# Raw weight loads on ScalarE's DMA queue, truer prices in the planner, and the last output tile in halves

## The chip, the cores and the metric

The kernel runs on one core of one Trainium2 chip. The metric is the device time of one execution in microseconds; three runs of the kernel before took 892.23, 892.72 and 895.94 us, so its median is 892.72. A core has TensorE (PE in the profile: matmuls from SBUF into PSUM; PEld is its weight load), VectorE (DVE), ScalarE (ACT), GpSimd (POOL) and SyncE (SP, which here only issues DMAs). All work in parallel, each through its own instructions in order; semaphores tie them together.

## The reference

Three blocks in a row, all in fp32. The attention output of 4 x 576 = 2304 tokens and 512 channels is the input of a gated feed-forward, and that one's output is the input of a second feed-forward.

```python
scores = (q @ k.T) / 8                   # 4 batches, 8 heads, 576 x 576, head width 64
# heads 0-3: a key counts if 0 <= i - j < 32; heads 4-7: if j <= i and j % 32 == i % 32
attn = softmax(where(mask, scores, -1e9)); x = attn @ v          # x: 2304 x 512
xn = x / sqrt(mean(x * x) + 1e-6) * rms_g
g = xn @ w_gate                          # 512 x 1536
x = (g * sigmoid(g) * (xn @ w_val)) @ w_out                      # 1536 x 512
h = x @ w_in                             # 512 x 2048
return (max(h, 0) + log1p(exp(-abs(h)))) @ w_out2                # 2048 x 512
```

The weights arrive as 64-bit floats, which the kernel reads as raw 64-bit words.

## The kernel before

**Attention.** Heads are taken in pairs, and a pair's queries in two units. For each pair one DMA loads queries and keys (`qk`, line 550) and one the values (`vb`, line 564). A unit's scores are matmuls on 64 rows of the array (lines 590 and 603), then come the maximum on VectorE (618), the exponentials on ScalarE (646, 650, 654), sums and reciprocals on VectorE (664 to 666), a transpose on TensorE (692), its eviction (292 on ScalarE or 289 on VectorE) and the product with the values (746). Only two `vb` and three `qk` buffers exist, so a load waits until TensorE has read the old content.

**Weights.** Every 128 x 512 block of raw 64-bit words is loaded into one of two `raw` buffers (`decode`, line 389) and made into fp32: ScalarE converts the high words (390), ScalarE or VectorE the low ones (391 or 393), VectorE joins them in two steps (395, 398). There are 74 such blocks, 512 KB each. Most results are stored to DRAM (`w_kept`, 402) and fetched again later (405). Each fp32 block is split into a rounded part (428, 448 on ScalarE) and a rest (374 on VectorE, 375 on GpSimd); a product of two split operands takes three matmuls (`mm3`, line 457).

**Feed-forwards.** Token columns are cut into chunks of 512 (the last of 256). The products of the first feed-forward run between the attention matmuls; later parts use a scheme of seven products for a 2 x 2 block. `out1` (994) and `out2` (1012) add products into the token store `xs`; the last round of `out2` stores each 128 x 512 output tile (1014).

**Order.** Nothing here is executed in the order of the program text. Each operation is added to a list with an engine, a price in ns and what it reads and writes; an alternative engine has its own price. `Trial.run` plays the list through with these prices, `emit` takes the best of 8 such trials by its own count, and the instructions of all engines are issued in the order of the begin times found there. A different price thus changes the order of everything behind it. A raw load counts as work of the engine SP in this plan (`dma`, line 298: 650 ns), and `AHEAD` and `FAR` hold back loads. TensorE's work has kinds (`mode`: 0 full matmuls, 1 and 3 on a part of the rows, 2 transposes); `LEAVE` is the number of ns by which other work must be more urgent before TensorE leaves the kind it is in for another, except between 0 and 2, where `LEFT` counts.

Of the kernel before, what the change touches and what calls it, by code (L numbers as in the profile page):

```python
# [16 lines left out]
AF = mybir.ActivationFunctionType  # L17
ALU = mybir.AluOpType
# [38 lines left out]
FAR, AHEAD = 12000, 1000  # L57
TURNS, KEEP, SWITCH, LEAVE = 8, 0.5, 125, 4000

# [199 lines left out]
def attn_glu_softplus(  # L259
# [113 lines left out]
    def two(eng, n, name, o, x, y, r, w):  # L373
        pr.add("DVE", 68 + n / 0.96, lambda: getattr(nc.vector, name)(o, x, y), r, w,  # L374
               alt=(110 + n * 2.3, lambda: getattr(nc.gpsimd, name)(o, x, y)))

# [5 lines left out]
    def decode(src, t, kt, keep):  # L382

        raw, kraw = raws.next()
        u, ku = cvu.next()
        words = raw.bitcast(U32).rearrange("p (n two) -> p n two", two=2)
        wlo, whi = words[:, :, 0], words[:, :, 1]
        quarters = raw.bitcast(U16).rearrange("p (n four) -> p n four", four=4)
        dma(340, lambda: nc.sync.dma_start(out=raw, in_=src), hold, [kraw])
        act(512, lambda: nc.scalar.activation(t, whi.bitcast(F32), AF.Copy, scale=2.0 ** -112), [kraw], [kt])  # L390
        pr.add("ACT", 15 + 512 / 0.98, lambda: nc.scalar.activation(  # L391
            u, quarters[:, :, 1], AF.Identity, bias=low, scale=2.0 ** -13), [kraw, all_of("eps")], [ku], alt=(68 + 512 / 1.5,
            lambda: nc.vector.tensor_scalar(out=u, in0=wlo, scalar1=29, scalar2=None,
                                            op0=ALU.logical_shift_right)))
        dve(512, lambda: nc.vector.scalar_tensor_tensor(
            out=u, in0=t.bitcast(U32), scalar=0x80000000, in1=u, op0=ALU.bitwise_and, op1=ALU.bitwise_or),
            [kt, ku], [ku])
        dve(512, lambda: nc.vector.scalar_tensor_tensor(  # L398
            out=t.bitcast(U32), in0=t.bitcast(U32), scalar=3, in1=u,
            op0=ALU.logical_shift_left, op1=ALU.bitwise_or), [kt, ku], [kt])  # L400
        if keep >= 3 * AGAIN:
            dma(170, lambda: nc.sync.dma_start(out=wk[keep], in_=t), [kt], [("wk", keep, keep + 1)])
# [4 lines left out]
    def prep_in(i, rows, sums, all4, eng):  # L407
# [25 lines left out]
        if sums:  # L433
            q = [(w32[:, k * 256:(k + 1) * 256], ("w32", k * 256, k * 256 + 256)) for k in range(4)]
            for o, name, a, b in ((3, "tensor_add", 2, 3), (2, "tensor_sub", 0, 2), (0, "tensor_sub", 3, 0),
                                  (1, "tensor_sub", 1, 0)):
                two("DVE", 256, name, q[o][0], q[a][0], q[b][0], [q[a][1], q[b][1]], [q[o][1]])
            part(1024, 512, 1024, eng)
            part(1024, 0, 512, eng)
# [67 lines left out]
    def attention(at, use):  # L507
# [62 lines left out]
        def stage_s(u):  # L570
# [51 lines left out]
            elif not late(u):  # L622
                dve(6, lambda: nc.vector.tensor_scalar(out=m, in0=m, scalar1=-SCALE, scalar2=None, op0=ALU.mult),
                    [km], [km])
# [13 lines left out]
        def stage_e(u):  # L638
# [8 lines left out]
            else:  # L647
                for a in range(n):
                    if mid(u):
                        pr.add("ACT", 60 + nk / 0.98, lambda a=a: nc.scalar.activation(  # L650
                            ev[:, a, :], sv[:, a, :], AF.Exp, bias=m[:, a:a + 1], scale=SCALE),
                            [kb_, km, all_of("table")], [(ke[0], a * nk, a * nk + nk)])
                        continue
# [8 lines left out]
        def stage_p(u, n, nk, loc, t0, e, ke, ev, z, kz):  # L662
            if whole(u) or mid(u):
                dve(n * nk, lambda: nc.vector.reduce_sum(out=z, in_=ev, axis=AX.X), [ke], [kz], lock=False)
            dve(6, lambda: nc.vector.tensor_scalar_add(out=z, in0=z, scalar1=1e-9), [kz], [kz])
            dve(30, lambda: nc.vector.reciprocal(out=z, in_=z), [kz], [kz], lock=False)
# [40 lines left out]
        def turned(xb, kx, n, nq):  # L707
            xv = xb[:, :n * 65].rearrange("p (a c) -> p a c", c=65)
            z, (kz, _, _) = mz.next()
            z, kz = z[:, 1, :n], (kz, 0, 10)  # L710
            dve(6, lambda: nc.vector.tensor_scalar_add(out=z, in0=xv[:, :, 64], scalar1=1e-9), [kx], [kz])
            dve(30, lambda: nc.vector.reciprocal(out=z, in_=z), [kz], [kz], lock=False)
# [283 lines left out]
    def out2(fs, g, first, c, j, last):  # L996
        ti = CUTS[c] // 128 + j
        ts = slice(j * 128, (j + 1) * 128)
        pb, kp = o_banks.next()
        pairs = []  # L1000
        for f in fs:
            i = f % 4
            st, km = g[f, c]
            pairs.append(([x[:, ts] for x in st], [wout[i][:, x, :] for x in (0, 1)],
                          lambda a, b, i=i, km=km: [(f"wout{i}", b * 512, b * 512 + 512), km[a]]))
        mm3(pb, kp, pairs, DM)
        o = ti * DM
        x, kx = xs[:, o:o + DM], ("xs", o, o + DM)
        if first:
            act(DM, lambda: nc.scalar.activation(x, pb, AF.Copy), [kp], [kx])  # L1010
        else:
            dve(DM, lambda: nc.vector.tensor_add(x, pb, x), [kp, kx], [kx])  # L1012
        if last:
            dma(256, lambda: nc.sync.dma_start(out=out[ti * 128:(ti + 1) * 128, :], in_=x),
                [kx], [("out", ti, ti + 1)])

# [320 lines left out]
```

## Time and profile before

| | |
|---|---|
| median of three runs | 892.72 us (892.23 to 895.94) |
| the profiled execution | 897.35 us, its span 895.6 us |
| TensorE matmuls | busy 880.6 us (98%) |
| VectorE | busy 717.6 us (80%) |
| ScalarE | busy 509.8 us (57%) |
| GpSimd | busy 62.9 us (7%) |
| DMA | 102.31 MB, mean 114 GB/s, all on one queue but 0.9 MB |

The span is from the first to the last instruction of the program; the execution's time has a little around it. Busy time of TensorE is modelled from pipelined matmuls, so a busy TensorE can still be slowed down, by a low granted clock for one. Register, branch, semaphore and DMA-issuing instructions do not count as busy: SyncE has no busy time at all, and its waits are seen in its issues. A wait in a row stands in square brackets: how long the engine was idle and what ended it.

### The profile page before, as it was taken

What the parts mean: (1) busy time and instruction counts of PE and PEld (TensorE: products, weight loads), DVE (VectorE), ACT (ScalarE), POOL (GpSimd) and SP (SyncE); (2) the same over time, 40 slices, a digit from 0 to 9 for tenths busy, and PEclk for the clock granted to TensorE, in tenths of its full rate; (3) what the DMA queues carried; (4) which work ended last, traced back from release to release, by engine and by line L of the source; (5) the groups of instructions that cost most, each with busy time, mean ns of one, the idle gap of its engine ahead of it and who ended that gap; (6) DMA issues with size and microseconds to landing.
All of it is one profiled execution on the core that took longest, in us unless ns stands there. A gap on an engine that the chain in (4) does not pass through costs nothing.

```text
span 895.6 us, 14064 instructions
## 1 busy us (share of the span) xinstructions
PE 880.6 (98%) x5350; PEld 729.5 (81%) x5350; DVE 717.6 (80%) x1326; ACT 509.8 (57%) x967; POOL 62.9 (7%) x59
## 2 busy tenths in 40 slices
PE   8889999999999999999999999999999999999998
PEld 7667778787878888888888888887888888888886
DVE  5988999897699997888899798977799457676644
ACT  3977766664364677565665478544473655434331
POOL 1210212310012000000000010000000000000000
PEclk8989999999999999999999999999999999999999
DMA  7764766533211246454542025311114111101003
GB/s 250 257 192 151 222 220 210 178 123 107 64 66 48 83 150 217 155 172 166 171 138 90 3 96 196 131 48 48 48 48 157 31 48 48 48 29 42 1 1 118
DMA packets 40996, 102.31 MB, mean 114 GB/s; under 512 B 4704, under 2 KB 5472, under 8 KB 40928
## 3 DMA queue, kind: packets, MB, share of 16 engines
q1 hardware_dynamic: 40928, 101.41, 35.0%
q8 instruction: 42, 0.69, 0.3%
q14 instruction: 26, 0.21, 0.1%
HBM read 80.42 MB, written 20.97 MB: 113 GB/s over the span
## 4 chain that ended last, share of the span: by engine, by line
PE 88%; DVE 6%; DMA 3%; ACT 1%; issue 1%; SPq 0%; DVEq 0%; ACTq 0%
PE bank L457 83%; PE bank L746 2%; PE bank L692 2%; PE bank L603 1%; DVE xs L994 1%; DMA vb<-v_loc 1%; DVE xs L374 1%; DVE tb L374 1%; DMA id_sb<-ident 1%; DVE gv L374 1%; PE bank L481 1%; DMA w<-w_kept 1%; DMA w_kept<-cvtx 0%; DVE gl L374 0%; PE bank L590 0%
## 5 line engine op out<-in xcount | busy, mean ns | idle before, releaser
L457 PE MATMUL bank<-ob,win 128*128 128x512 f32 (+1 forms) x1560 | 432.9, 361 | 1.0 <-ACT win L428 0.5
L457 PEld LDWEIGHTS bank<-ob,win 128*128 128x128 f32 x1560 | 284.5, 189 | 53.7 <-ACT win L428 1.6
L457 PE MATMUL bank<-tb,win 128*128 128x512 f32 x672 | 231.2, 393 | 1.0 <-DVE gv L909 0.5
L457 PEld LDWEIGHTS bank<-tb,win 128*128 128x128 f32 x672 | 125.1, 188 | 23.9 <-DVE gv L909 1.3
L1012 DVE TENSOR_TENSOR xs<-bank,xs 128x512 f32<-128x512 f32 x126 | 86.9, 691 | 42.9 <-PE bank L457 41.1
L428 ACT ACTIVATE win<-w 128x512 fp32r<-128x512 f32 (+1 forms) x136 | 82.9, 614 | 54.0 <-DVE w L374 20.6
L374 DVE TENSOR_TENSOR win<-w,win 128x512 fp32r<-128x512 f32 (+1 forms) x128 | 85.1, 670 | 19.5 <-ACT win L428 17.2
L457 PE MATMUL bank<-wout,ghx 128*128 128x512 f32 x304 | 99.9, 389 | 0.0
L457 PE MATMUL bank<-wout,gh 128*128 128x512 f32 x272 | 90.3, 389 | 0.0
L457 PE MATMUL bank<-ghx,wout 128*128 128x512 f32 x224 | 83.2, 393 | 0.0
L457 PE MATMUL bank<-gh,wout 128*128 128x512 f32 (+1 forms) x256 | 79.2, 351 | 0.8 <-DVE xs L994 0.8
L994 DVE TENSOR_TENSOR xs<-bank,xs 128x512 f32<-128x512 f32 (+1 forms) x100 | 62.6, 633 | 10.9 <-PE bank L457 9.9
L457 PEld LDWEIGHTS bank<-wout,ghx 128*128 128x128 f32 x304 | 56.9, 188 | 11.7
L457 PEld LDWEIGHTS bank<-wout,gh 128*128 128x128 f32 x272 | 50.9, 188 | 10.5
L457 PE MATMUL bank<-wout,glx 128*128 128x512 f32 x152 | 53.2, 389 | 0.0
L457 PEld LDWEIGHTS bank<-gh,wout 128*128 128x128 f32 x256 | 45.5, 189 | 8.2 <-DVE xs L994 1.3
L457 PEld LDWEIGHTS bank<-ghx,wout 128*128 128x128 f32 x224 | 41.9, 188 | 9.0 <-issue 0.2
L457 PE MATMUL bank<-wout,gl 128*128 128x512 f32 x136 | 47.7, 389 | 0.0
L391 ACT ACTIVATE cvu<-raw,low 128x512 uint32<-128x512 uint16 x47 | 35.7, 760 | 19.0 <-DVE cvtx L398 9.0
L905 ACT ACTIVATE gv<-bank 128x512 f32<-128x512 f32 x48 | 28.5, 594 | 31.6 <-PE bank L457 29.4
L909 DVE TENSOR_TENSOR gv<-bank,gv 128x512 f32<-128x512 f32 x48 | 33.1, 690 | 16.4 <-PE bank L457 7.9
L374 DVE TENSOR_TENSOR w<-w 128x256 f32<-128x256 f32 x107 | 45.1, 421 | 0.9
(161 smaller groups left out, 1278.7 us busy)
## 6 DMA issues: line engine op xcount, KB each, us to landing
raw<-w SPq DMA_DIRECT2D x74, 512.0 KB, 3.9
w<-w_kept SPq DMA_DIRECT2D x52, 256.0 KB, 2.7
w_kept<-cvtx SPq DMA_DIRECT2D x25, 256.0 KB, 2.9
cvt<-w_kept SPq DMA_DIRECT2D x25, 256.0 KB, 2.8
w_kept<-w SPq DMA_DIRECT2D x20, 256.0 KB, 2.7
qk<-qk SPq DMA_DIRECT2D x8, 601.0 KB, 5.5
out<-xs SPq DMA_DIRECT2D x18, 256.0 KB, 2.0
w_kept<-cvt SPq DMA_DIRECT2D x17, 256.0 KB, 2.1
```

Source lines behind the costliest of these rows:

```text
L374: pr.add("DVE", 68 + n / 0.96, lambda: getattr(nc.vector, name)(o, x, y), r, w, alt=(110 + n * 2.3, lambda: getattr(nc.gpsimd, name)(o, x, ...
L391: pr.add("ACT", 15 + 512 / 0.98, lambda: nc.scalar.activation(u, quarters[:, :, 1], AF.Identity, bias=low, scale=2.0 ** -13), [kraw, all_o ...
L428: act(n, lambda: nc.scalar.activation(h, t, AF.Copy), [kt], [reg(0, o + lo, o + hi)])
L457: lambda a=a, b=b, i=i, st=st, mv=mv: nc.tensor.matmul(o, lhsT=st[a], rhs=mv[b], start=(first and i == 0), stop=(last and i == m - 1), ski ...
L481: pr.add("PE", 4 * n / 2.4, lambda i=i, y=y: nc.tensor.matmul(p, lhsT=ones, rhs=y, start=c == 1 and i == 3 or i == 0, stop=c >= 2 or i == ...
L603: nc.tensor.matmul(sp[o, a * nk:(a + 1) * nk], lhsT=qt[r, c:c + 64], rhs=qt[r, QW + c:QW + c + nk], start=False, stop=True, skip_group_che ...
L692: pr.add("PE", 108, lambda a=a, a0=a0, tp=tp: nc.tensor.transpose(tp[:kp, a * 128:a * 128 + 128], pv[:, a0 + a, :], id_sb), [kpv, all_of(" ...
L746: pr.add("PE", 59 if loc else 36, lambda a=a, h=h, o=o, t=t: nc.tensor.matmul(xb[64 * h:64 * h + 64, a * nq:(a + 1) * nq], lhsT=vt[r0:r1, ...
L905: act(CH, lambda: nc.scalar.activation(o, y[0], AF.Copy), [y[1]], [ko])
L909: dve(CH, lambda: nc.vector.tensor_add(o[0], y[0], o[0]), [y[1], o[1]], [o[1]])
L994: dve(n, lambda: nc.vector.tensor_add(x, pb, x), [kp, kx], [kx])
L1012: dve(DM, lambda: nc.vector.tensor_add(x, pb, x), [kp, kx], [kx])
```

## The change

Raw loads (line 389) are issued by ScalarE. In the planner they still count as SP's work. All other DMAs stay with SyncE. Several prices change: an elementwise operation on GpSimd, ScalarE's conversion of low words, VectorE's two joining steps, the sums of weight blocks, tiny operations on VectorE, and exponentials of line 650. `LEAVE` falls from 4000 to 3000. The last output tile is computed, added and stored in two halves of 256 columns.

```diff
-TURNS, KEEP, SWITCH, LEAVE = 8, 0.5, 125, 4000
+TURNS, KEEP, SWITCH, LEAVE = 8, 0.5, 125, 3000
...
-               alt=(110 + n * 2.3, lambda: getattr(nc.gpsimd, name)(o, x, y)))
+               alt=(180 + n * 2.4, lambda: getattr(nc.gpsimd, name)(o, x, y)))
...
-        dma(340, lambda: nc.sync.dma_start(out=raw, in_=src), hold, [kraw])
+        dma(340, lambda: nc.scalar.dma_start(out=raw, in_=src), hold, [kraw])
...
-        pr.add("ACT", 15 + 512 / 0.98, lambda: nc.scalar.activation(
+        pr.add("ACT", 180 + 512 / 0.98, lambda: nc.scalar.activation(
             u, quarters[:, :, 1], AF.Identity, bias=low, scale=2.0 ** -13), [kraw, all_of("eps")], [ku], alt=(68 + 512 / 1.5,
...
-        dve(512, lambda: nc.vector.scalar_tensor_tensor(
+        dve(560, lambda: nc.vector.scalar_tensor_tensor(
             out=t.bitcast(U32), in0=t.bitcast(U32), scalar=3, in1=u,
...
-            dve(6, lambda: nc.vector.tensor_scalar_add(out=z, in0=z, scalar1=1e-9), [kz], [kz])
+            dve(50, lambda: nc.vector.tensor_scalar_add(out=z, in0=z, scalar1=1e-9), [kz], [kz])
...
-        pb, kp = o_banks.next()
-        pairs = []
...
+        cuts = (0, DM // 2, DM) if last and ti == NT // 128 - 1 else (0, DM)
+        for n0, n1 in zip(cuts, cuts[1:]):
+            n = n1 - n0
+            pb, kp = o_banks.next()
+            pb = pb[:, :n]
...
+            if last:
+                dma(n // 2, lambda x=x, n0=n0, n1=n1: nc.sync.dma_start(
+                    out=out[ti * 128:(ti + 1) * 128, n0:n1], in_=x), [kx], [("out", 2 * ti + (n0 > 0), 2 * ti + 1 + (n1 == DM))])
```

How the order moves, at three places. In its rows a name with a number is a tile (`raw_79` and `raw_80` are the two raw buffers, `vb_114` and `vb_115` the two value buffers), and `x5` is a repetition.

ScalarE, where the seventh raw block is loaded, in the second half of the dense attention stretch (`win_90` are split weights, `eb` exponentials, `sq` squares, `cvtx` a block being converted):

```order
-L292 ACTIVATE xs<-bank_75 128x14x14
+L428 ACTIVATE win_90<-w_83 128x512
+L650 ACTIVATE eb_121<-bank_72,mz_132 128x54 x2
+L389 DMA raw_79<-w 128x512
+L650 ACTIVATE eb_121<-bank_72,mz_132 128x54 x4
 L792 ACTIVATE sq_131<-bank_75 128x56
 L390 ACTIVATE cvtx<-raw_80 128x512
 L369 ACTIVATE ob<-xs,rg_sb 128x512
```

The raw load stands between ScalarE's own instructions, behind a split of weights and two exponentials.

SyncE at the same place of the program, first before, then now (`qk` are queries and keys):

```order
L389 DMA raw_79<-w 128x512 [waits DMAHW5_49,DVE_49,Activation_49]
L389 DMA raw_80<-w 128x512 [waits DMAHW7_49,Activation_49]
L550 DMA qk_110<-qk 128x1202 [waits DMAHW3_49,PE_49]
L389 DMA raw_79<-w 128x512 [waits DMAHW1_49,DMAHW4_49,DVE_49,Activation_49]
L564 DMA vb_114<-v_loc 96x1170 [waits PE_49]
L564 DMA vb_115<-v_str 128x780 [waits DMAHW6_49,PE_49]
L550 DMA qk_111<-qk 128x1216 [waits PE_49]
```

```order
L550 DMA qk_112<-qk 128x1216 [waits DMAHW7_49]
L550 DMA qk_110<-qk 128x1202 [waits PE_49]
L564 DMA vb_114<-v_loc 96x1170 [waits DMAHW4_49,PE_49]
L564 DMA vb_115<-v_str 128x780 [waits DMAHW6_49,DMAHW5_49,PE_49]
L550 DMA qk_111<-qk 128x1216 [waits DMAHW3_49,PE_49]
```

The three raw loads are gone from SyncE's row, and the value load stands right behind the attention load.

TensorE just behind, where those values are read (`ob,win_90` are products of tokens and weights, `id_sb,eb` transposes, `pt,vb` products with values):

```order
 L603 MATMUL bank_71<-qk_111 64x54 x10
-L457 MATMUL bank_72<-ob,win_90 128x512 x5
+L746 MATMUL bank_76<-pt_126,vb_114 64x64 x6
+L746 MATMUL bank_76<-pt_127,vb_114 64x64 x4
+L457 MATMUL bank_72<-ob,win_90 128x512
 L692 MATMUL bank_73<-id_sb,eb_120 96x128 x3
 L692 MATMUL bank_74<-id_sb,eb_120 96x128
-L457 MATMUL bank_72<-ob,win_90 128x512 x2
-L746 MATMUL bank_76<-pt_126,vb_114 64x64 x6
```

The products with `vb_114` stood behind seven weight matmuls and four transposes; now they stand ahead of them.

## Rows read from the trace of the kernel before

**Rows 1.** The page: busy time of the engines, and TensorE's granted clock in 40 slices.

```profile
PE 880.6 (98%) x5350; PEld 729.5 (81%) x5350; DVE 717.6 (80%) x1326; ACT 509.8 (57%) x967; POOL 62.9 (7%) x59
...
PEclk8989999999999999999999999999999999999999
```

**Rows 2.** Stretches: length, PE, PEld, DVE, ACT, POOL busy, clock, DMA share, GB/s.

```profile
18.00:54.00 36.00, 31.35 (x526) 24.07 (x524) 33.57 (x100) 33.63 (x119) 5.11 (x5) 1.00 0.83 264
54.00:72.00 18.00, 16.37 (x131) 13.18 (x132) 13.43 (x25) 13.47 (x27) 3.67 (x4) 0.81 0.32 100
72.00:275.00 203.00, 201.82 (x1491) 161.72 (x1490) 180.11 (x340) 122.64 (x210) 33.69 (x28) 1.00 0.47 150
275.00:875.00 600.00, 598.84 (x2920) 504.28 (x2919) 473.19 (x824) 333.62 (x602) 18.07 (x15) 1.00 0.28 89
```

**Rows 3.** Timeline of TensorE, 26 to 36 us: start, us, instruction, [idle before].

```profile
31.66 1.98 PE L481 MATMUL bank<-gv,ones 128*128 128x512 f32 x4 [0.90 <-DVE xs L289]
33.48 0.27 PE L692 MATMUL bank<-id_sb,eb 128*96 128x128 f32 x1
34.27 0.73 PE L457 MATMUL bank<-ob,win 128*128 128x512 f32 x2 [0.51 <-ACT win L428]
34.84 0.49 PE L692 MATMUL bank<-id_sb,eb 128*96 128x128 f32 x3
```

**Rows 4.** Timeline of TensorE, 45 to 63 us.

```profile
46.28 0.34 PE L746 MATMUL bank<-pt,vb 96*64 96x64 f32 x4 [0.38 <-DVE pt L289]
...
50.12 1.43 PE L457 MATMUL bank<-ob,win 128*128 128x512 f32 x5 [0.29 <-ACT eb L650]
...
52.18 0.71 PE L457 MATMUL bank<-ob,win 128*128 128x512 f32 x2
55.23 2.21 PE L746 MATMUL bank<-pt,vb 96*64 96x64 f32 x36 [2.35 <-DMA vb<-v_loc]
```

**Rows 5.** Timeline of SyncE, 41 to 59 us.

```profile
46.64 0.33 SPq L389 DMA_DIRECT2D raw<-w  x1
47.02 0.42 SPq L564 DMA_DIRECT2D vb<-v_loc  x1
```

**Rows 6.** Stretches around the low clock; columns as in rows 2.

```profile
51.00:55.00 4.00, 1.66 (x9) 0.79 (x7) 3.68 (x11) 3.98 (x11) 0.69 (x1) 0.98 0.94 250
55.00:61.50 6.50, 6.27 (x46) 5.32 (x47) 3.65 (x9) 3.37 (x7) 1.68 (x3) 0.50 0.49 139
```

**Rows 7.** Line 389, to 72 us and to 275 us: ns min/median/max of an issue.

```profile
L389 SPq DMA_DIRECT2D raw<-w x8: 327/328/1491, 19.3 to 58.6; - x8
...
L389 SPq DMA_DIRECT2D raw<-w x30: 327/328/444, 72.4 to 246.6; - x30
```

**Rows 8.** Conversion of low words on ScalarE (line 391) and VectorE (line 393).

```profile
L391 ACT ACTIVATE cvu<-raw,low x47: 738/763/781, 41.8 to 574.1; 128x512 uint32<-128x512 uint16 x47
...
L393 DVE TENSOR_SCALAR cvu<-raw x27: 381/421/1098, 28.5 to 562.9; 128x512 uint32<-128x512 uint32 x27
```

**Rows 9.** Line 564, all value loads: time from issue to landing.

```profile
DMA to landing us min/median/max: 2.9/4.5/8.1
```

**Rows 10.** DMA issues: count, KB each, median us to landing.

```profile
out<-xs SPq DMA_DIRECT2D x18, 256.0 KB, 2.0
...
vb<-v_loc SPq DMA_DIRECT2D x8, 438.8 KB, 4.9
```

**Rows 11.** Timeline of TensorE, 97 to 100 us: a change between kinds of matmul.

```profile
98.50 0.39 PE L457 MATMUL bank<-ob,win 128*128 128x512 f32 x1
98.72 0.39 PE L457 MATMUL bank<-glx,wout 128*128 128x512 f32 x1
99.04 0.95 PE L746 MATMUL bank<-pt,vb 54*64 54x54 f32 x44
```

**Rows 12.** Groups of VectorE: mean ns of one; adds of 512 and 256 columns.

```profile
L1012 DVE TENSOR_TENSOR xs<-bank,xs 128x512 f32<-128x512 f32 x126 | 86.9, 691 | 42.9 <-PE bank L457 41.1
...
L994 DVE TENSOR_TENSOR xs<-bank,xs 128x256 f32<-128x256 f32 x20 | 8.1, 421 | 1.9 <-PE bank L457 1.5
```

More of the change, by code (lines that the diff above doesn't have):

```diff
@@ L394, in decode @@
                                             op0=ALU.logical_shift_right)))
-        dve(512, lambda: nc.vector.scalar_tensor_tensor(
+        dve(560, lambda: nc.vector.scalar_tensor_tensor(
             out=u, in0=t.bitcast(U32), scalar=0x80000000, in1=u, op0=ALU.bitwise_and, op1=ALU.bitwise_or),
             [kt, ku], [ku])
-        dve(512, lambda: nc.vector.scalar_tensor_tensor(
+        dve(560, lambda: nc.vector.scalar_tensor_tensor(
             out=t.bitcast(U32), in0=t.bitcast(U32), scalar=3, in1=u,
@@ L436, in prep_in @@
                                   (1, "tensor_sub", 1, 0)):
-                two("DVE", 256, name, q[o][0], q[a][0], q[b][0], [q[a][1], q[b][1]], [q[o][1]])
+                two("DVE", 285, name, q[o][0], q[a][0], q[b][0], [q[a][1], q[b][1]], [q[o][1]])
             part(1024, 512, 1024, eng)
@@ L622, in stage_s @@
             elif not late(u):
-                dve(6, lambda: nc.vector.tensor_scalar(out=m, in0=m, scalar1=-SCALE, scalar2=None, op0=ALU.mult),
+                dve(50, lambda: nc.vector.tensor_scalar(out=m, in0=m, scalar1=-SCALE, scalar2=None, op0=ALU.mult),
                     [km], [km])
@@ L649, in stage_e @@
                     if mid(u):
-                        pr.add("ACT", 60 + nk / 0.98, lambda a=a: nc.scalar.activation(
+                        pr.add("ACT", 130 + nk / 0.98, lambda a=a: nc.scalar.activation(
                             ev[:, a, :], sv[:, a, :], AF.Exp, bias=m[:, a:a + 1], scale=SCALE),
@@ L710, in turned @@
             z, kz = z[:, 1, :n], (kz, 0, 10)
-            dve(6, lambda: nc.vector.tensor_scalar_add(out=z, in0=xv[:, :, 64], scalar1=1e-9), [kx], [kz])
+            dve(50, lambda: nc.vector.tensor_scalar_add(out=z, in0=xv[:, :, 64], scalar1=1e-9), [kx], [kz])
             dve(30, lambda: nc.vector.reciprocal(out=z, in_=z), [kz], [kz], lock=False)
@@ L998, in out2 @@
         ts = slice(j * 128, (j + 1) * 128)
-        pb, kp = o_banks.next()
-        pairs = []
[L1001 to L1015, printed above, removed]
+        cuts = (0, DM // 2, DM) if last and ti == NT // 128 - 1 else (0, DM)
[3 more added lines that the diff above has]
+            pb = pb[:, :n]
+            pairs = []
+            for f in fs:
+                i = f % 4
+                st, km = g[f, c]
+                pairs.append(([x[:, ts] for x in st], [wout[i][:, x, n0:n1] for x in (0, 1)],
+                              lambda a, b, i=i, km=km, n0=n0, n1=n1: [(f"wout{i}", b * 512 + n0, b * 512 + n1), km[a]]))
+            mm3(pb, kp, pairs, n)
+            o = ti * DM + n0
+            x, kx = xs[:, o:o + n], ("xs", o, o + n)
+            if first:
+                act(n, lambda x=x, pb=pb: nc.scalar.activation(x, pb, AF.Copy), [kp], [kx])
+            else:
+                dve(n, lambda x=x, pb=pb: nc.vector.tensor_add(x, pb, x), [kp, kx], [kx])
+            if last:
+                dma(n // 2, lambda x=x, n0=n0, n1=n1: nc.sync.dma_start(
+                    out=out[ti * 128:(ti + 1) * 128, n0:n1], in_=x), [kx], [("out", 2 * ti + (n0 > 0), 2 * ti + 1 + (n1 == DM))])
     def xv(kk, c):
```

## The prediction, made before the change was run

> **What bounds the kernel now.** I read the head of the page first: TensorE is busy for 880.6 of 895.6 us, and its granted clock is full in nearly every slice but two near the start [rows 1]. Busy time can hide stalls, so the next view is the table of stages [rows 2]. From 72 us to 875 us TensorE is idle for 1.18 + 1.16 = 2.3 us in 803. By taking waits away there the change can win 2.3 us and no more. From 18 to 72 us it is idle for 4.65 + 1.63 = 6.3 us. There ScalarE is busy for 33.63 of 36 us and VectorE for 33.57, so up to 54 us the two vector engines set the pace and TensorE waits for them. Among its waits there are 0.90 us on an eviction and 0.51 us on split weights [rows 3], and the longest, 2.35 us on a load of attention values that ended at 55.23 us [rows 4]; that load was issued at 47.02 [rows 5], so it took 8.1 us, the most that any such load took [rows 9]. Right after that wait the granted clock is 0.50, the lower of its two levels, for 6.5 us, after a stretch in which TensorE was busy for 1.66 of 4 us [rows 6].
>
> The profiled execution took 897.35 us around its span of 895.6. The three timed runs have their median at 892.72, 4.6 us lower, and one run at 895.94. Half of the 6.27 busy us at half clock is 3.1 us, most of that difference. So I read the two lower runs as runs without the slow stretch, and do not count its end as a gain on the median. I make the sum as a difference and put it on 892.72; on the profiled time it gives the same difference below 897.35, with the stretch left in.
>
> **The change part by part.**
>
> *Raw loads move to ScalarE.* An issue took 0.33 us on SyncE; there are 8 up to 72 us and 30 from there to 275 us [rows 7]. No issue by ScalarE is in the trace. From below an issue costs nothing (the sequencer issues beside a running activation), from above 0.33 us and the end of the activation it waits for, up to 0.76 us [rows 8]. I take the 0.33 us of the same instruction on SyncE. Seven issues stand ahead of the first change of table after the start, which ends the dense stretch: 7 x 0.33 = 2.3 us. In the same stretch the new order has three conversions of low words (line 391) on ScalarE where the old one has one: 2 x 0.76 = 1.5 us more, while VectorE sheds 2 x 0.42 = 0.8 [rows 8]. ScalarE's slack from 18 to 54 us is 36 - 33.63 = 2.4 us, so 3.8 - 2.4 = **+1.4 us** reaches TensorE (between 0 and 3.8). From 72 to 275 us ScalarE has 203 - 122.6 = 80 us free [rows 2], and 30 x 0.33 = 10 us disappear in that. What is queued behind an issue on ScalarE is every split and eviction that TensorE waits for; the rival below is about that.
>
> *The value load behind the wait.* In the old order SyncE issued a raw load at 46.64 and the value load at 47.02 [rows 5]. In the new one the raw load stands on ScalarE behind a split of weights and two exponentials, so the values go first, behind one attention load. The old reading of that buffer ended at 46.62 (46.28 + 0.34) [rows 4], so the raw load did not hold the issue up by more than 0.4 us; it held up the bytes. Other loads of this tensor took 4.9 us in the median, and 2.9 to 8.1 with the other value tensor's [rows 9, 10]. With 4.9 the values land at 51.9. But the new TensorE order has less to do meanwhile: the seven matmuls of 50.12 to 52.89 and the four transposes between them [rows 4] now stand behind the values, not ahead of them. TensorE comes to the values at 50.12, waits 1.8 us, and still has 2.5 us of that work to do: 51.9 + 2.5 = 54.4 against 55.23, **-0.8 us**. With a landing in 2.9 us the whole wait goes (-2.35); with 8.1 us it is +2.4. The median is the nearest row.
> The Trainium skill has a rule that speaks against the change here: "DMA: Bandwidth & Descriptors", section "Issuing engines are not separate DMA queues", says that loads from SyncE and ScalarE share the same 16 DMA engines and interleave, so that a second issuer saves issue time alone. By it only the order of the issues would count, which is how I have counted. The same page's section "Queues, rings and completion order" says that each DMA engine takes turns between the two issuers' rings packet by packet; by that a raw load issued a moment earlier would delay the values by their own size at most. No row here shows two issuers, and neither changes the sum.
>
> *Truer durations.* VectorE's and ScalarE's work is the same in number; the planner's dearer prices change the order alone. First, the five transposes that stood around the first weight matmuls now stand ahead of the statistics (line 481). Of their work 0.27 + 0.49 us [rows 3] can fill the gaps of 0.90 and 0.51 us: **-0.7 us** (0 if the probabilities they read are late). Second, half of the 2.3 us of waits after 72 us: **-1.2 us** (from -2.3; above zero is the rival).
>
> *LEAVE 4000 to 3000.* TensorE's order changes between kinds of matmul (full, transpose, row-tiled) 113 times before and 105 times now. From the last weight matmul at 98.72 to the value matmul at 99.04 it is 0.32 us, against 0.22 between two weight matmuls [rows 11]: 0.1 us a change, **-0.8 us** (between 0 and -1.6).
>
> *The last tile in halves.* The add at the end takes 0.42 us for 256 columns, as other adds of that width do, not 0.69 [rows 12]; the first half is added and stored beside the second half's matmuls. A store takes 2.0 us at full size [rows 10]; I leave that (at best -0.5 for half the bytes). Twelve half matmuls replace six for the same columns: from 0, if the columns alone count, to 6 x 0.22 = +1.3 us, if a half one took as long as a whole one [rows 11]; I take 0, since the halves change nothing but the columns of each. **-0.3 us** (-0.8 to +1.0).
>
> *SyncE without raw loads.* Stores of kept weights and attention loads stood behind them. TensorE's one long wait on a load after the start is the one counted above, so nothing else is gained: 0.
>
> Sum: +1.4 - 0.8 - 0.7 - 1.2 - 0.8 - 0.3 = **-2.4 us**, 892.72 - 2.4 = **890.3 us** (profiled, with a slow stretch, 895.0). Its own range, with the bounds that matter, is 887 to 895.
>
> **The rivals.**
>
> *A. The early stage opens up: 886 us.* The value wait goes whole (-2.35), ScalarE's issues cost nothing (0 instead of +1.4), every wait after 72 us goes (-2.3), the rest as above (-1.8): 892.72 - 6.4 = 886.3; 883.1 if the median of before holds a slow stretch that goes as well. For it: the planner's price of the line 391 conversion was 200 ns under its 763 [rows 8], so the old order ran ahead of itself just where the vector engines are full. Against it: the new order gives ScalarE more work there.
>
> *B. ScalarE is held at its issues: 898.7 us.* A raw load may only go when its buffer has been read. In the new order 22 of the 74 issues wait for VectorE and 20 for an earlier DMA, and 13 of the first 31 wait for VectorE. Where VectorE is behind the plan, ScalarE stands still with all splits behind it, and VectorE then waits for those in turn. From 72 to 275 us VectorE is busy for 180.1 of 203 us [rows 2] and TensorE for all but 1.2. Price: an instruction of VectorE, about 0.7 us, at 13 issues is 9 us, of which two thirds pass on, 6 us: 898.7. It decides as soon as TensorE's idle time in that stage goes above some 5 us. Against it: ScalarE's 80 us free.
>
> *C. The value wait grows: 896.6 us.* TensorE comes to it earlier with less work; if the values land after 8 us again, +2.4 in place of -0.8, and if that brings the slow clock back in most runs, +3.1: 890.3 + 3.2 + 3.1 = 896.6.
>
> *D. The second queue and the order do nothing that can be told: 892.7 us.* Every term above is a us or so and some may cancel.
>
> **How the numbers follow.** About 0.5% (4.5 us) is what a measurement of this kernel can tell from no change: below 888.3 is faster, above 897.2 slower. Chances: forecast 0.40, A 0.37, B 0.13, C 0.06, D 0.04. The forecast and D lie within 0.5%; A is faster; B is slower, C half of each. So faster 0.37, no change 0.47, slower 0.16. A comes close to the forecast, since three of its terms need only be at their better ends and the slow clock would add to it. The range reaches from A's lower time to just over B's: 883 to 899.
>
> **What would show it.** Right: the page has two rows for raw loads and the rest, with ScalarE's issues at about 0.33 us; the value wait near 51 us is shorter than 2.35 us; TensorE's idle time from 18 to 54 us stays between 3 and 6 us, and ScalarE is fuller there. The span's end has a VectorE add of 0.42 us. Wrong for A: ScalarE's stretch to the table change grows. Wrong for the forecast: TensorE idle by over 5 us from 72 to 875 us (B), or under 2 us from 18 to 72 us (A). If the granted clock stays full around 55 us while the median does not move, my reading of the 3.7 us between the runs was right.

## The result, and the profile of the changed kernel

The changed kernel is slower: 903.48 us in the median of four runs (900.99 to 910.16) against 893.81 of the kernel before (four runs, 892.23 to 895.94), a ratio of 1.0113 with a 95% interval of 1.008 to 1.0145. In a later measurement it had 902.65 against 893.64 us, 1.0094 (1.0067 to 1.0121). The forecast was 890.3, the range 883 to 899. The profiled execution took 904.33 us, its span is 902.5.

The page answers to [rows 1]. Below the clock stand two of its rows on DMA queues; the second is new:

```profile
PE 882.8 (98%) x5356; PEld 730.9 (81%) x5356; DVE 717.0 (79%) x1318; ACT 512.4 (57%) x978; POOL 61.8 (7%) x57
...
PEclk7899999999999999999999999999999999999999
...
q1 hardware_dynamic: 30416, 62.61, 21.5%
q10 hardware_dynamic: 10656, 38.80, 13.4%
```

The work is the same, on every engine within 3 us of before. So the 7 us more in the span are waits and a low clock. The stretches answer to [rows 2], same columns:

```profile
18.00:54.00 36.00, 31.09 (x528) 24.89 (x525) 30.89 (x83) 29.31 (x101) 3.53 (x3) 0.89 0.67 225
54.00:72.00 18.00, 16.35 (x177) 11.84 (x176) 17.12 (x41) 17.72 (x48) 1.90 (x3) 1.00 0.60 185
72.00:275.00 203.00, 198.40 (x1453) 157.88 (x1451) 177.08 (x332) 123.01 (x215) 27.98 (x23) 1.00 0.45 148
275.00:875.00 600.00, 599.16 (x2915) 505.07 (x2916) 471.76 (x821) 335.39 (x605) 26.01 (x22) 1.00 0.29 90
```

TensorE's idle time from 72 to 875 us was 2.3 us and is 4.60 + 0.84 = 5.4; 4.45 of it lie between 220 and 280 us. That stretch alone, first of the kernel before, then of the changed one:

```profile
220.00:280.00 60.00, 59.17 (x298) 47.88 (x297) 49.45 (x81) 29.78 (x48) 8.82 (x7) 1.00 0.19 61
```

```profile
220.00:280.00 60.00, 55.55 (x275) 44.48 (x275) 44.05 (x72) 27.57 (x45) 6.96 (x5) 0.97 0.24 79
```

0.83 us idle became 4.45, and with them came a clock of 0.97. The timeline of TensorE has two waits there, and the granted clock behind the second is 0.53, near the lower level (the last two rows are stretches):

```profile
255.36 0.50 PE L457 MATMUL bank<-gh,wout 128*128 128x512 f32 x1 [1.45 <-DVE gv L488]
...
275.44 2.08 PE L457 MATMUL bank<-ob,win 128*128 128x512 f32 x4 [3.00 <-DVE gv L958]
```

```profile
271.00:275.40 4.40, 1.44 (x7) 0.86 (x5) 4.40 (x9) 3.15 (x7) 1.03 (x1) 0.98 0.00 0
275.40:278.80 3.40, 3.37 (x8) 2.69 (x9) 3.40 (x6) 1.86 (x4) 1.76 (x2) 0.53 0.35 101
```

VectorE, which TensorE waits for, was late since it had itself waited for ScalarE. The timeline of ScalarE shows why ("ACTq" is its sequencer, which issues the DMAs):

```profile
240.96 0.63 ACT L960 ACTIVATE gvx<-gvx 128x512 f32<-128x512 f32 x1 [4.85 <-DVE gvx L958]
242.35 0.63 ACT L945 ACTIVATE ghx<-gvx 128x512 fp32r<-128x512 f32 x1 [0.76 <-DVE gvx L961]
242.35 0.82 ACTq L389 DMA_DIRECT2D raw<-w  x2
245.99 0.75 ACT L391 ACTIVATE cvu<-raw,low 128x512 uint32<-128x512 uint16 x1 [3.00 <-DMA raw<-w]
```

and in VectorE's timeline the wait that follows from it:

```profile
247.32 0.69 DVE L395 SCALAR_TENSOR_TENSOR cvu<-w,cvu 128x512 uint32<-128x512 uint32 x1 [3.61 <-ACT w L390]
```

The two raw loads, blocks 34 and 35 of 74, wait for nothing of their own: their buffers were free at 215.3 and 218.5 us, when their last reader ended. But in ScalarE's row they stand behind two instructions that wait for VectorE (4.85 and 0.76 us), and only when the second has been let go are they issued, 27 and 24 us late, and ScalarE then waits 3.00 us for the bytes. In the kernel before, SyncE issued the same two at 212.5 and 213.0 us, right behind a store of its own (212.10); they landed at 216.4 and 217.7, some 23 us ahead of their first readers (239.43 and 240.64). ScalarE has the same two waits there, but the loads don't stand behind them; rows of SyncE, then of ScalarE:

```profile
212.10 0.32 SPq L402 DMA_DIRECT2D w_kept<-cvt  x1
212.51 0.89 SPq L389 DMA_DIRECT2D raw<-w  x2
```

```profile
237.23 0.63 ACT L960 ACTIVATE gvx<-gvx 128x512 f32<-128x512 f32 x1 [4.17 <-DVE gvx L958]
238.89 0.63 ACT L945 ACTIVATE ghx<-gvx 128x512 fp32r<-128x512 f32 x1 [1.02 <-DVE gvx L961]
239.43 0.66 ACT L390 ACTIVATE w<-raw 128x512 f32<-128x512 f32 x1
```

All issues of line 389 in the changed kernel, who waited for their bytes (us, times), and their landing, beside [rows 7]; the median issue is as long as on SyncE:

```profile
L389 ACTq DMA_DIRECT2D raw<-w x74: 333/334/1658, 21.4 to 573.3; - x74
...
  ACT w L390: 6.8, 3
  ACT cvu L391: 3.0, 1
...
DMA to landing us min/median/max: 3.2/3.9/8.8
```

Early in the program one more wait looked like a cause. SyncE's load of `rms_g` (2 KB) had moved from 5.71 us to behind five attention loads; these are rows of the changed kernel's timelines of SyncE, ScalarE and TensorE:

```profile
21.13 0.42 SPq L1127 DMA_DIRECT2D rg_sb<-rms_g  x1
```

```profile
29.15 0.72 ACT L369 ACTIVATE ob<-xs,rg_sb 128x512 fp32r<-128x512 f32 x1 [1.25 <-DMA rg_sb<-rms_g]
```

```profile
33.39 0.61 PE L590 MATMUL bank<-mask 64*64 64x480 bf16 x2 [2.56 <-ACT eb L654]
...
56.77 0.63 PE L746 MATMUL bank<-pt,vb 96*64 96x64 f32 x14 [1.01 <-DMA vb<-v_loc]
```

The last row is the value wait of [rows 4]: 1.01 us, not 2.35.

### The profile page after: what moved, and what is told of

Read it like the earlier page. It is cut to its first block, busy times and chain, and to the rows that moved or that the text cites. A ratio compares the mean times of both kernels' runs of the same rounds, so it can differ in the third digit from the quotient of the medians.

```text
span 902.5 us, 14066 instructions
## 1 busy us (share of the span) xinstructions
PE 882.8 (98%) x5356; PEld 730.9 (81%) x5356; DVE 717.0 (79%) x1318; ACT 512.4 (57%) x978; POOL 61.8 (7%) x57
## 4 chain that ended last, share of the span: by engine, by line
PE 88%; DVE 5%; DMA 3%; ACT 2%; issue 1%; SPq 0%; ACTq 0%
PE bank L457 84%; DMA raw<-w 1%; PE bank L603 1%; PE bank L746 1%; PE bank L692 1%; DMA id_sb<-ident 1%; DMA rg_sb<-rms_g 1%; DVE xs L374 1%; DVE xs L994 1%; PE bank L481 1%; DVE tb L374 0%; DVE cvu L395 0%; DVE gv L374 0%; PE bank L590 0%; DVE win L374 0%
## 5 line engine op out<-in xcount | busy, mean ns | idle before, releaser
L1016 DVE TENSOR_TENSOR xs<-bank,xs 128x512 f32<-128x512 f32 (+1 forms) x127 | 86.9, 686 | 48.1 <-PE bank L457 46.6
L457 PE MATMUL bank<-wout,gh 128*128 128x512 f32 (+1 forms) x276 | 90.5, 387 | 0.0
L994 DVE TENSOR_TENSOR xs<-bank,xs 128x512 f32<-128x512 f32 (+1 forms) x100 | 62.5, 633 | 15.8 <-PE bank L457 14.5
L457 PE MATMUL bank<-wout,gl 128*128 128x512 f32 (+1 forms) x138 | 48.0, 386 | 0.0
L391 ACT ACTIVATE cvu<-raw,low 128x512 uint32<-128x512 uint16 x50 | 38.0, 760 | 13.0 <-DVE cvtx L398 5.4
```

The lines of the kernel that those rows point to most:

```text
L391: pr.add("ACT", 180 + 512 / 0.98, lambda: nc.scalar.activation(u, quarters[:, :, 1], AF.Identity, bias=low, scale=2.0 ** -13), [kraw, all_ ...
L457: lambda a=a, b=b, i=i, st=st, mv=mv: nc.tensor.matmul(o, lhsT=st[a], rhs=mv[b], start=(first and i == 0), stop=(last and i == m - 1), ski ...
L994: dve(n, lambda: nc.vector.tensor_add(x, pb, x), [kp, kx], [kx])
L1016: dve(n, lambda x=x, pb=pb: nc.vector.tensor_add(x, pb, x), [kp, kx], [kx])
```

## The experiments

Theories: **Q**, the two loads held in ScalarE's row; **R**, the late load of `rms_g`; **O**, the planner's new order (prices and LEAVE) is worse in itself; **S** and **T**, the cost lies in the number of ScalarE's issues, or in two issuers at once. In the table the ratio is to runs of the kernel before beside it (23 to 35 of them). "Idle" is TensorE's idle time from 220 to 280 us; "early" the start of the ninth change of table on ScalarE (line 302, where it loads another set of functions), "rest" the span from there to its end. All three are from the one profiled execution. Behind that point all kernels have the same work (3019 to 3021 weight matmuls of 512 columns, two of 256 counted as one).

| kernel | median us | ratio (95%) | idle | early | rest |
|---|---|---|---|---|---|
| before (profiled) | | | 0.83 | 189.2 | 706.4 |
| changed, first runs | 903.48 | 1.0113 (1.008 to 1.0145) | 4.45 | 192.3 | 710.2 |
| changed, again | 902.65 | 1.0094 (1.0067 to 1.0121) | 5.06 | 190.6 | 711.7 |
| 1 before, all raws on ScalarE | 895.40 | 1.0023 (0.9998 to 1.0047) | 3.23 | 186.2 | 707.8 |
| 2 before, only the two on ScalarE | 896.92 | 1.0034 (1.0014 to 1.0055) | 2.73 | 184.7 | 710.2 |
| 3 before, all but the two on ScalarE | 893.05 | 1.0012 (0.9986 to 1.0039) | 0.64 | 182.5 | 704.6 |
| 4 changed, the two on SyncE | 896.98 | 1.0043 (1.0017 to 1.0069) | 1.26 | 188.8 | 705.4 |
| 5 changed, all raws on SyncE | 896.04 | 1.0027 (1.0002 to 1.0053) | 0.94 | 190.2 | 706.3 |
| 6 changed, rms_g early | 900.90 | 1.0083 (1.0057 to 1.0109) | 3.69 | 186.7 | 708.3 |
| 7 changed, rms_g early, the two on SyncE | 894.56 | 1.0031 (1.0004 to 1.0057) | 1.49 | 186.6 | 706.3 |
| 8 changed, rms_g early, all raws on SyncE | 896.54 | 1.0032 (1.0008 to 1.0057) | 0.93 | 186.8 | 706.3 |
| 9 before, LEAVE 3000 | 895.16 | 1.0022 (0.9999 to 1.0045) | 0.84 | 187.6 | 705.4 |
| 10 before, new prices | 894.30 | 1.0003 (0.9986 to 1.0021) | 1.40 | 186.1 | 706.5 |
| 11 changed, LEAVE 4000, the two on SyncE | 893.71 | 0.999 (0.9971 to 1.0008) | 1.41 | 187.9 | 706.0 |
| 12 before, last tile in halves | 891.68 | 0.9977 (0.9954 to 1.0001) | 0.81 | 186.2 | 704.8 |
| 13 as 3, with halves | 893.40 | 0.9999 (0.998 to 1.0018) | 1.31 | 187.5 | 708.3 |
| 14 halves, first eight raws on ScalarE | 892.35 | 0.998 (0.9959 to 1.0) | 0.77 | 183.4 | 704.7 |

**The queue (1 to 3, and 4).** Number 1 is the kernel before with one word changed:

```
-        dma(340, lambda: nc.sync.dma_start(out=raw, in_=src), hold, [kraw])
+        dma(340, lambda: nc.scalar.dma_start(out=raw, in_=src), hold, [kraw])
```

> The kernel before, with raw loads issued by ScalarE and nothing else changed; plan, prices and order of all other work as before. Theory Q (the queue): an issue in ScalarE's row cannot run ahead of ScalarE's own work. In the kernel before, SyncE issued the two raw loads of 212.5 and 213.0 us 23 us ahead of their first reader; with the changed kernel ScalarE issued the same two at 242.4 and 242.7, 27 us after their buffer was free, and the reader had to wait. By Q this kernel shows the same: these two issues near 240 us, TensorE idle by 3 to 5 us from 220 to 280 us, and a time 4 to 6 us above before (ratio 1.005 to 1.007). The load of rms_g stays early here, so no stall near 33 us. Theory O (the order: prices and LEAVE alone make it slower): the same time as before within 2 us. Theory T (two issuers disturb each other's transfers): raw loads land later than before in the median (4.0 us before), and the loss is spread over the stretch to 275 us.

It issued the two loads at 235.96 and 236.33 us, 32 and 29 us after their buffers were free; TensorE lost 3.23 us. That is Q's picture, but not Q's size: +2.1 us where Q said 4 to 6, and the interval ends at 1.0047. In its profile the kernel is 3 us ahead of before up to there; whether that is the change or chance isn't shown. Raw loads landed in 3.7 us in the median, so nothing speaks for T.

Number 2 gives ScalarE these two loads alone, number 3 all others, number 4 takes them from the changed kernel (the counter `raws.k` runs from 0):

```
2  lambda e=nc.scalar if raws.k in (33, 34) else nc.sync: e.dma_start(out=raw, in_=src)
3, 4  lambda e=nc.sync if raws.k in (33, 34) else nc.scalar: e.dma_start(out=raw, in_=src)
```

Of number 2: 

> The reverse: the kernel before with just two of 74 raw loads on ScalarE, those of 212.5 and 213.0 us; the others stay on SyncE, order of all other work as before. Theory Q: these two are enough. They are issued near 238 us, behind ScalarE's waits, ScalarE waits about 3 us for them, TensorE is idle for 3 to 4 us from 220 to 280 us against 0.8 before, ratio 1.002 to 1.005. Theory S (the cost is in the number of issues, or in two issuers at once): no change, 0.999 to 1.001.

Of number 3: 

> The kernel before with 72 of its 74 raw loads on ScalarE and the two of 212.5 and 213.0 us on SyncE; order of all other work as before. With all 74 on ScalarE it was 2.1 us slower (ratio 1.0023), its two loads were issued at 236.0 and 236.3 us, 32 us after their buffer was free, and TensorE lost 3.2 us from 220 to 280 us; up to 186 us it was 3 us ahead of the profiled kernel before (table change at 186.24 against 189.18 us). Theory Q: the loss goes and what is ahead stays, so 2 to 4 us under all 74, ratio to before 0.996 to 1.000: faster by up to 3 us. Theory S (issues cost by their number): as all 74, 1.002 or more.

Of number 4: 

> The changed kernel with only two of its 74 raw loads (the two that ScalarE issued at 242.4 and 242.7 us) given back to SyncE; order of everything else the same. Theory Q: SyncE issues them as soon as their buffers are free, near 216 and 219 us; ScalarE's wait of 3.00 us at 243 goes, statistics of that stage come some 3 to 5 us earlier, TensorE's stalls at 253 and 272 us (1.45 and 3.0 us) and the slow clock behind go: 4 to 6 us under the changed kernel, ratio to before 1.004 to 1.007, the same gain as with all raw loads back. Theory S (the cost is spread over all issues in ScalarE's row): 72 of 74 are still there, so under 1 us is gained.

Two issues of 74 are enough: number 2 is slower by 0.34%, with the interval clear of 1. Its timeline of ScalarE repeats that of the changed kernel, on another order of everything:

```profile
232.79 0.63 ACT L960 ACTIVATE gvx<-gvx 128x512 f32<-128x512 f32 x1 [4.17 <-DVE gvx L958]
234.45 0.63 ACT L945 ACTIVATE ghx<-gvx 128x512 fp32r<-128x512 f32 x1 [1.02 <-DVE gvx L961]
234.46 0.86 ACTq L389 DMA_DIRECT2D raw<-w  x2
238.09 0.67 ACT L390 ACTIVATE w<-raw 128x512 f32<-128x512 f32 x1 [3.01 <-DMA raw<-w]
```

and TensorE pays behind it:

```profile
248.31 0.50 PE L457 MATMUL bank<-gh,wout 128*128 128x512 f32 x1 [1.79 <-DVE gv L488]
```

The other 72 issues cost nothing that can be told: number 3 has 1.0012, and 7, with 72 issues on ScalarE, is as fast as 8 with none. Number 3 did not get ahead of before, as Q had hoped, and its gain on number 1 (1 us by the ratios) can't be told from nothing; against Q's cause it says nothing. Number 4 is the changed kernel with the two loads in SyncE's row and every other instruction in the order of the changed kernel; rows of SyncE, then of ScalarE:

```profile
218.18 0.87 SPq L389 DMA_DIRECT2D raw<-w  x2
```

```profile
238.87 0.63 ACT L945 ACTIVATE ghx<-gvx 128x512 fp32r<-128x512 f32 x1 [0.76 <-DVE gvx L961]
239.40 0.75 ACT L391 ACTIVATE cvu<-raw,low 128x512 uint32<-128x512 uint16 x1
```

ScalarE goes straight on, its 3.00 us wait is gone. The ratio falls from 1.0094 or 1.0113 to 1.0043, by 4.6 or 6.3 us, as Q said; the interval is clear of that of the first runs and just touches that of the later ones. The same edit on number 6 gives number 7: 1.0083 to 1.0031, 4.6 us, the intervals just touch. One stall of 1.26 us behind line 958 stays at 268 us, smaller than the 3.00. The column "rest" says the same by place: 707.8 to 711.7 us in the five kernels that hold the two loads (mean 709.6), 704.6 to 708.3 in the others (mean 705.9).

**The load of rms_g (6, 7, 8).**

```
-        dma(40, lambda: nc.sync.dma_start(out=id_sb, in_=ident), [], [all_of("id")])
-        dma(2, lambda: nc.sync.dma_start(out=rg_sb, in_=rg), [], [all_of("rg")])
+        dma(40, lambda: [nc.sync.dma_start(out=id_sb, in_=ident), nc.sync.dma_start(out=rg_sb, in_=rg)], [], [all_of("id")])
+        dma(2, lambda: None, [], [all_of("rg")])
```

Of number 6: 

> The changed kernel with the load of rms_g issued right behind that of the identity, near 4.5 us, and not behind five attention loads that wait for TensorE; the order of all other work is the same. Theory R: ScalarE no longer waits for it until 29.15 us, TensorE's 2.56 us stall at 33.4 us goes and with it the stretch at half clock behind it (6.8 us long, 3 us lost): 3 to 6 us under the changed kernel, ratio to before 1.005 to 1.008. If ScalarE is so full in this stretch that its other work is late anyway, at most 1 us is gained (ratio 1.010). The stalls at 253 and 272 us stay by every theory.

Of number 7: 

> The changed kernel with the load of rms_g early and two of the 74 raw loads given back to SyncE; 72 stay on ScalarE. By theories Q and R together nothing of the loss is left: ratio 0.998 to 1.001, against 1.0043 for the two loads alone and 1.0083 for rms_g alone. If 72 issues on ScalarE cost something by their number, it stays 2 us or more above the kernel with all raw loads back and rms_g early, which runs beside it.

Of number 8: 

> The changed kernel with both repairs: raw loads all back on SyncE, and the load of rms_g behind that of the identity. What is left of the change is the planner's prices, LEAVE and the halves. Raws back alone gave a ratio of 1.0027 to before, rms_g early alone 1.0083, the changed kernel 1.0113. Theory R (the late load of rms_g costs some 2.5 us by itself): 893.3 us, ratio 0.999 to 1.001. Theory O (the new order costs something of its own): no better than raws back alone, ratio 1.002 to 1.004. If the new order holds the gain that I forecast for it (some 3 us without the raw issues), ratio 0.996 to 0.998.

R's 3 to 6 us are not there. Number 6 has 1.0083 against 1.0113 and 1.0094 of the changed kernel, 7 has 1.0031 against 1.0043 of 4, and 8 is no faster than 5 (1.0032 against 1.0027): 1 us or so in the mean, which these intervals can't tell from nothing. The profile of 6 says why. With the load early the stall stays at half its size, since line 654 is late there anyway; in 4, 5, 7 and 8 it is 1.18 to 1.27 us, whether the load is late (4, 5) or early (7, 8):

```profile
27.77 0.39 PE L590 MATMUL bank<-mask 64*64 64x480 bf16 x2 [1.19 <-ACT eb L654]
```

And the changed kernel's second profile has it at 1.20 us, with the load landed at 26.03 and ScalarE reading it at 26.49 without a wait. There it was issued at 20.32 and took 5.7 us, not at 21.13 and 8.0: the other 1.4 us of the stall belong to one execution. One sign for R is left open: the ninth change of table comes at 186.6 to 186.8 us in the three kernels with the load early and at 188.8 to 192.3 in the four with it late, a larger step than the medians show.

**The order (5, 9, 10, 11, and the repetition).**

Number 5 is the changed kernel with line 389 on `nc.sync`; 9 is the kernel before with the one constant, 10 with the new prices alone; 11 is number 4 with the constant put back:

```
9   -TURNS, KEEP, SWITCH, LEAVE = 8, 0.5, 125, 4000
    +TURNS, KEEP, SWITCH, LEAVE = 8, 0.5, 125, 3000
11  -TURNS, KEEP, SWITCH, LEAVE = 8, 0.5, 125, 3000
    +TURNS, KEEP, SWITCH, LEAVE = 8, 0.5, 125, 4000
```

Of number 5: 

> The changed kernel with all raw loads issued by SyncE again; order of TensorE, VectorE, GpSimd and of ScalarE's other work as in the changed kernel. Theory Q: TensorE's stalls at 253 and 272 us go (4.3 us idle there and 1.7 us of a slow clock behind), so 5 to 6 us under the changed kernel; the stall behind the load of rms_g near 33 us stays, so still 2 to 5 us above before (ratio to before 1.002 to 1.006). Theory O: as slow as the changed kernel, 1.010 or more. Theory R (the late load of rms_g is the larger part): hardly better than the changed kernel, 1.008 or more, since that load stays where it is.

Of number 9: 

> The kernel before with LEAVE 3000 in place of 4000 and nothing else; the planner makes the order of all engines again. With the loads of the changed kernel repaired (raws on SyncE, rms_g early) prices, LEAVE and halves together still had a ratio of 1.0032 to before, and the halves alone 0.9977. Forecast on record for LEAVE: -0.8 us, from fewer changes between kinds of matmul. Theory L (LEAVE is what makes the new order worse): 1.003 to 1.006. Theory P (the prices do): 0.999 to 1.001.

Of number 10: 

> The kernel before with the new prices of the planner and nothing else: LEAVE 4000, raw loads on SyncE, last tile whole; rms_g is loaded early in its plan. Forecast on record for prices: -0.7 us (transposes ahead of the statistics) and -1.2 us (waits after 72 us), so a ratio of 0.998. Theory P: 1.003 to 1.006, with a wait of TensorE of 1 us or more behind VectorE's line 958 near 265 us, as in the kernels with the new order. Theory L: 0.998 to 1.001.

Of number 11: 

> The changed kernel with LEAVE back at 4000 and the two raw loads of 212.5 and 213.0 us on SyncE; prices, 72 raw loads on ScalarE and the halves stay. In this plan the load of rms_g stands early by itself. Theory L (LEAVE is the rest of the loss): 0.998 to 1.001, against 1.0031 for the kernel with LEAVE 3000 and both loads repaired. Theory P (the prices' order is worse in any case): 1.003 to 1.005. Theory X (each part is harmless and only the two together made this order): 0.999 to 1.002, not told from theory L here but for the single runs, where LEAVE alone had 1.0022.

Of the repetition: 

> The changed kernel as it is, beside the other two. Its first four runs gave a ratio of 1.0113 to before (1.008 to 1.0145). If that was not chance of the chip, again 1.008 to 1.014, with the two raw loads issued near 240 us and TensorE idle for 3.5 to 5 us from 220 to 280 us. If the repairs took back less than it seemed, because those four runs were slow ones, 1.005 to 1.008.

Number 5 came out as Q had it, and the repetition as the first runs. With both late loads repaired 0.3% stays (7 and 8). LEAVE back at 4000 takes that away, with the new prices, 72 raw loads on ScalarE and the halves still in: number 11 has 0.999. It differs from number 4 by that constant alone (1.0043, the intervals are clear of each other), though its new plan also loads `rms_g` early; from 7, where that load is early too, it differs by 0.4%, and the intervals just meet. So the lower LEAVE is the likely rest of the loss. The prices alone measure 1.0003, so theory P falls. LEAVE alone measures 1.0022, under the 1.003 to 1.006 of theory L and not clear of 1; that the harm needs both together (X) is not excluded. Two signs speak for X. A wait of TensorE of 0.93 to 1.49 us behind line 958, at 266 to 269 us, stands in 4, 5, 7 and 8 and in none of 9, 10 and 11. And TensorE's changes between full, row-tiled and transposing matmuls, counted in the traces by line, are 109 before, 109 with LEAVE alone, 108 with the prices alone and 101 with both.

Where the loss lies, the profiles don't show. "Rest" does not differ between 4, 5, 7, 8 and 9 to 11 (705.4 to 706.5 us). "Early" has a mean of 188.9 us in the seven kernels with LEAVE 3000 and new prices and of 185.7 in the seven with the order of before up to there (before, 1 to 3, 12 to 14), but those with `rms_g` early (186.6 to 186.8) are no later than 11 (187.9). Nor does TensorE's row from 18 to 54 us tell it, here in 11, then in 7, then in 9:

```profile
18.00:54.00 36.00, 31.74 (x535) 24.30 (x531) 31.68 (x96) 33.37 (x119) 6.00 (x7) 1.00 0.80 262
```

```profile
18.00:54.00 36.00, 30.08 (x454) 24.09 (x454) 32.08 (x91) 32.41 (x108) 4.67 (x5) 0.91 0.75 253
```

```profile
18.00:54.00 36.00, 33.11 (x562) 25.66 (x561) 33.94 (x99) 34.51 (x122) 6.11 (x7) 1.00 0.82 270
```

Number 7 is idle for 1.7 us more than 11, at a clock of 0.91; but 9, with the lower LEAVE too, is idle for less than either. Which reordering costs the time stays open, since executions differ by 2 us at the start alone (below).

**The halves, and a better kernel (12, 13, 14).** The edit of 12 is the diff's part in `out2`; 14 adds `nc.scalar if raws.k < 8 else nc.sync`.

Of number 12: 

> The kernel before with the last output tile in halves and nothing else; the plan of the last part is made again by that. I forecast -0.3 us for it (-0.8 to +1.0): a ratio of 0.999 to 1.001. A rival: twelve half-width matmuls cost what whole ones cost, +1.3 us. The end of the span would show an add of 0.42 us, and from the last matmul to the end some 0.3 us less than in the kernel before.

Of number 13: 

> A version that could beat both: the kernel before with 72 raw loads on ScalarE (the two of 212.5 and 213.0 us stay on SyncE) and the last tile in halves. The two parts alone had ratios of 1.0012 and 0.9977 to before. If both are what they measured, 0.999; if the early stage really gains from the second issuer (the profile of the first part was 887.0 us in its span, the shortest of all), 0.996 to 0.998; if issues by ScalarE cost by their number, 1.000 to 1.002.

Of number 14: 

> A version meant to beat both: the kernel before with the last tile in halves and only the first eight raw loads (to 72 us) on ScalarE. The halves alone had 0.9977. If the second issuer shortens the wait for values near 52 us (2.35 us before, 2.95 with the halves alone, 0.92 to 1.12 in the three kernels with 72 or 74 raw loads on ScalarE) and ScalarE's later issues are what took it back, 0.995 to 0.997. If the shorter wait is only moved to another place of the early stage, 0.997 to 0.999, as the halves alone.

From the last matmul to the end of the span it is 3.72 us before and 3.50 with the halves, and half matmuls cost half (starts at 886.97, 887.09, 887.21):

```profile
886.97 0.28 PE L457 MATMUL bank<-wout,gl 128*128 128x256 f32 x1
887.09 0.28 PE L457 MATMUL bank<-wout,gh 128*128 128x256 f32 x1
887.21 0.28 PE L457 MATMUL bank<-wout,gl 128*128 128x256 f32 x1
```

So the sum's 0.3 us was right within 0.1. The rest of 12's gain is not explained by that edit. 12 and 14 are the fastest kernels here, 0.2% under before, with intervals that end at 1, so a gain isn't shown for certain; 14 came out as its second case, the halves alone, and in 13 (0.9999) a second issuer for 72 loads adds no gain.

## Why the prediction was wrong

**The step that failed first is "Raw loads move to ScalarE".** I priced an issue at its own 0.33 us (it took 0.334 in the median) and let "30 x 0.33 = 10 us disappear" in ScalarE's 80 free us from 72 to 275. ScalarE's free time is made of waits, and an issue behind a waiting instruction waits with it: two issues went 27 and 24 us after their buffers were free, and TensorE was idle for 4.45 us from 220 to 280 us in place of 0.83. I should have asked, for each moved load, how far ahead of its reader SyncE had issued it, and what stands before it in the new row. The two loads with 23 us of lead in the old trace and two waiting instructions ahead of them in the new row could have been found before the run; the same two waits, 4.17 and 1.02 us, stand in the old trace. The runs put 5 to 6 of the 8 to 10 us on these two issues (changed against 4) and some 4 on LEAVE or on LEAVE with the prices (7 against 11). Of the +1.4 us in the dense stretch the runs show nothing: its end, the first change of table after the start, comes at 52.1 to 54.3 us in the order of before with the early raw loads on SyncE (before, 2, 12) and at 51.3 to 56.3 with them on ScalarE (1, 3, 13, 14). "SyncE without raw loads: 0" looked at who had stood behind the loads, not at what the loads lose by leaving a row that waits for little. The Trainium skill has the rule, in "PSUM — Partial Sum Buffer", section "Engine vs sequencer instructions": the queues of ScalarE, VectorE and GpSimd are strictly first in, first out. The rows at 242.35 us agree. The Trainium skill's page that I cited, "DMA: Bandwidth & Descriptors", section "Issuing engines are not separate DMA queues", says that a second issuer saves only time on the sequencer; here it cost 3.7 us in the rest of the span, and the rule does not tell of that.

**Rival B** had the right end and half of the mechanism: slower, decided by idle time over 5 us from 72 to 875 us (5.4 measured), 898.7 against 903.5. It had ScalarE stand still at an issue whose buffer is not free; in fact the buffer had been free for 27 us, and the issue stood behind ScalarE's own waits. The issues that do wait for VectorE cost nothing that can be told (number 3).

**"LEAVE 4000 to 3000: -0.8 us" has the wrong sign beside the new prices.** I counted eight fewer changes of kind at 0.1 us each; taking LEAVE back gained some 4 us (1.0031 to 0.999). **"Truer durations: -0.7 and -1.2"**: new prices alone are 1.0003 (0.9986 to 1.0021), so -1.9 us (0.9979) lies just outside what was measured, and nothing is nearer. TensorE's waits from 72 to 875 us did not halve either: 2.5 us in number 10 against 2.3 before. Both were forecasts of an order from a count of rows; what an order does hangs on what is late, and the count didn't show it.

**The value load** was forecast at -0.8 us; the waits went that way, but no more is shown. In the order of before the wait is 2.35 us (2.95 in 12) with raws on SyncE and 0.75 to 1.12 in 3, 13 and 14 with the early raws on ScalarE; in 1 TensorE doesn't wait for the values at all (its 0.92 us there is an eviction). But it is 0.38 in 2, whose early raws are on SyncE, so an execution's chance is as large. In the new order it is 3.06 and 3.44 with raws on SyncE (8, 5), and with them on ScalarE 1.01 and 1.96 in the changed kernel's two profiles and 2.08 to 2.30 in 4, 6 and 7: about -1.3 in the mean, but from a larger wait. **The halves** were right at the end of the span (0.22 us for 0.3). **Rival A** fell: the time rose.

**The clock.** I read the 4.6 us between the profiled execution and the median as a slow stretch. The 35 runs of before beside numbers 1, 4, 5 and 6 bear it out: 889.2 to 890.8 us in those with a mean clock of 1.000, 896.7 to 898.1 at 0.992. The changed kernel's six later runs had a mean clock of 0.9910, before beside them 0.9951; at 0.75 to 0.96 us for each 0.001, as the runs of before have it, some 3 to 4 of its 9 us are clock. From 220 to 280 us, behind the waits, it lost 1.8 us of that in both profiles (0.97 over 60 us); the rest lies before 72 us, where executions of before lose some too.

## What to carry to other kernels

A DMA moved to a compute engine's queue keeps its price but loses its lead: it is issued no sooner than everything ahead of it in that row has been let go, so list, for each moved load, the lead it had and the waits now ahead of it. Leave on a queue that waits for little the loads that are issued long before their reader. And take a stall out and measure before calling it a cause: of the most conspicuous early stall here half belonged to one execution, and the other half stayed when its supposed cause was gone.

## What the runs showed of the hardware

- A DMA issue in ScalarE's row does not wait for the activation ahead of it to end: both start at 242.35 us, and the two issues (0.82 us) run beside it. It does wait until that activation's own wait is over.
- Runs of one kernel on one core spread by 1% (888.97 to 898.10 us, 35 runs), and mean granted clock carries most of it: of a standard deviation of 2.7 us a straight line through clock and time leaves 1.0. A mean of 0.999 means 0.2% of the time, 1.8 us, at the lower of the two levels, so 0.9 us lost; 0.75 to 0.96 were measured.
- The fifth attention load was issued at 3.06 us to within 0.01 in 15 of the 17 profiled executions (in 10 and 11 at 3.5) and landed at 7.8 to 10.1 us in them. TensorE waits for it, so single profiles differ by some 2 us before 11 us. It landed at 7.8 to 8.8 in the three kernels with `rms_g` early and at 9.5 to 10.1 in the four with it late, but at 8.1 to 10.1 in the order of before; that it is all chance isn't shown.
- After the 3.00 us wait TensorE ran at 0.53 for 3.4 us; it had been busy for 1.44 of 4.40 us.
